# Order of the first loads, repeated-row loads for three vectors, and another place for batch 1's k, in a fused linear-attention and MLP-mixer kernel

## The chip, the cores and the metric

One core of one Trainium2 chip runs the whole program. The metric is the device time of one execution in microseconds (us), as the median of several runs.

## The reference

Linear attention without softmax over 8 batches, 8 heads, 576 tokens and 64 features a head, normalized to its root mean square, then a residual mixer (ResMLP with affine norms) with d_model 512 and a hidden width of 2048. Inputs and output are float32.

```python
kv = einsum('bhsd,bhse->bhde', k, v)
out = einsum('bhsd,bhde->bhse', q, kv)
x = out / sqrt(mean(out * out, -1) + 1e-6) * g_norm      # heads side by side: [b, s, 512]
a1 = alpha1 * x + beta1
tok = einsum('ts,bsd->btd', w_tok, a1)
u = x + lam * tok
a2 = alpha2 * u + beta2
ch = maximum(a2 @ w_ch1, 0) @ w_ch2
result = u + lam * ch
```

## The kernel before

**How the work is tiled.** Tokens lie on partitions, 128 at a time; 576 tokens make four tiles and a tail of 64, and the tails of two neighbouring batches share one tile (`xt`). Weights are cast to bf16 as they are loaded and stay in SBUF: `wt` is W_tok transposed, `w1` W_ch1 in four blocks of 512 hidden columns (L890 multiplies with it, a ReLU on ACT follows, L885), `w2` W_ch2 in four blocks (L915). These two, with `tok` (L789), are the main work of TensorE (PE): for each batch 16 groups of four L890, then 16 groups of four L915.

**Two streams on PE.** `mm` (L110) puts each group of matmuls in the list `main` (the two MLP layers, in fixed order) or `fill` (all the rest: attention, token mixing, transposes, for the batches to come). `schedule` (L122) is a planner written in the kernel: every operation has a cost that its author gave it, every load a size, and the planner runs a small model of five engines and one shared DMA stream. At each time it takes, on ACT, DVE, POOL and SP, the first operation by priority (`P.bias`, `pri`) that is ready in the model, and on PE a `fill` group if one is ready, woven matmul by matmul with a `main` group. What comes out is one fixed order for each engine (`self.sequence`), and `synchronize` (L257) puts semaphore waits where they are needed. On the chip every engine works through its order strictly: an instruction that waits holds up all behind it on its engine.

**Batch 0, the head of the program.** No main work is ready yet, so batch 0 is done in four pairs of heads. For each pair p: SP loads raw k and q (L486), POOL loads v, cast to the matmul type float32r (L478); POOL rounds k (`round_early`, L563) and copies q (`qt_early`, L574); PE transposes q (L580), ACT evicts it (L586); PE forms kv (`kv_early`, L613), DVE and ACT copy it into `kvc` (L624, L627); PE forms the output (`norm_pair`, L745, and the tail of 64 tokens in `norm_tail`, L764, for two pairs together). `norm_ops` follows: square on ACT (L695), reduce on DVE (L698), square root on ACT (L701), reciprocal on DVE (L704), and three DVE multiplications (L706 by the reciprocal, L710 into `rm` or `rtl`, which token mixing reads, L713 into `xt`); for the pairs the copy to `xm` is on ACT (L716) and its product with g_norm on POOL (L718). PE then mixes tokens (`tok_pair`, L804, 20 matmuls a pair), DVE adds (L812), PE transposes for the MLP (`a2_pair`, L843), and ACT applies alpha2 and beta2 on the way out (L847). The first main matmul needs all four pairs of this.

**Constants.** W_tok is loaded by POOL (L504, L506) after v of pair 0, and transposed on PE (L955, L957). Column sums of W_tok (L976, L978) spread beta1's part over rows. Six rows (alpha1, lam, beta1, alpha2, beta2, g_norm) are loaded by ACT's queue into one partition, in this order (L495, L497). DVE forms e1 = alpha1 * lam * g_norm * 8 and lam * beta1 there (L525 to L536). A row is spread over 128 partitions by a matmul with K=1 against a row of ones and an ACT copy: `broadcast` (L544, L547) for e1, g_norm, lam, alpha2 and beta2, `beta_rows` (L994, L998) for lam * beta1. A float32 matmul counts twice in the trace (two passes).

**Batch 1.** Its q and k are loaded by SP in two halves each, by the same `load_early`: k into the region of W_ch2 (`w2`), where batch 0's k was, q into `xm[2:4]`. ACT rounds this k (L566), POOL copies q. `w2` can be loaded (L1054) when those roundings are done. v of batch 1 follows on POOL's queue (`load_v(1, 0, 8)`), when PE has finished with batch 0's. Later batches are loaded by `load_kv` and `load_q`.

Of the kernel before, what the change touches and what calls it, by code (L numbers as in the profile page):

```python
# [17 lines left out]
DM = 512  # L18
# [34 lines left out]
class Prog:  # L53
    ENGINES = ("PE", "ACT", "DVE", "POOL")

    def __init__(self, nc, stack):
        self.nc, self.stack = nc, stack
        self.ops, self.lastw, self.readers = [], {}, {}
        self.ps = stack.enter_context(nc.psum_tensor("ps", [128, 8, 512], F32))
        self.eng = {"PE": nc.tensor, "ACT": nc.scalar, "DVE": nc.vector,  # L60
                    "POOL": nc.gpsimd, "SP": nc.sync}
        self.pools = {"main": (0, 1, 2, 3), "fill": (4, 5, 6, 7), "any": tuple(range(8))}
        self.main, self.fill = [], []
        self.bias = 0.0
        self.reach = 24

    def bank(self, pool):
        return Bank(self, pool)
# [41 lines left out]
    def mm(self, stream, cols, fns, r=(), w=(), slow=False, after=(), margin=0.3,  # L110
           urgent=False):

        n = len(fns)
        per = cols * MM_NS + 0.0025
        o = Op("PE", "w" if slow else "m", n * (max(per, 0.213 if slow == "r" else 0.109) if slow else max(per, 0.056)),
               0.24, fns, self.bias, len(self.ops))
        o.margin, o.narrow, o.urgent = 0.0 if urgent else margin, cols < 512, urgent
        (self.main if stream == "main" else self.fill).append(o)
        return self._add(o, r, w, after)


    def schedule(self):  # L122
# [50 lines left out]
        def take(o, t, cost=None):  # L173
            nonlocal dma_free, left
            for tile, b in zip(o.alloc, place(o, t)):
                tile.bank = b
                if owner[b] is not None:
                    o.deps.update(owner[b].ops)
                owner[b] = tile
            o.start = t  # L180
            if o.kind == "d":
                if o.nbytes > 0.25:
                    dma_free = max(dma_free, t + 1.4) + o.nbytes
                    o.end = dma_free + 1.6
                else:
                    o.end = t + 3.2
            else:
                o.end = t + (o.cost if cost is None else cost) + o.lat
            events.add(o.end)
            if o.margin:  # L190
                events.add(o.end + 0.3)
            left -= 1

        while left:
            moved = True
            while moved:
# [13 lines left out]
                if free["PE"] <= t + 1e-9:  # L210
                    m = main[0] if main and can(main[0], t) else None
                    f = None
                    for o in fill[:self.reach]:
                        if o.urgent or not (last_fill and m):
                            if can(o, t, o.margin if m else 0.0):
                                f = o
                                break
                    last_fill = False
                    if f is not None and m is not None and f.kind == "w" and m.narrow:
                        f = None  # L220
                    if f is not None and m is not None and f.kind == "w" and not f.urgent and not any(
                            x.pool == "any" for x in f.alloc):
                        fill.remove(f)
                        main.pop(0)
                        cost = sum(max(len(o.fns) * 0.056, (len(o.fns) * 0.075 if o is f else o.cost))
                                   for o in (f, m))
                        take(f, t, cost)
                        take(m, t, cost)
                        free["PE"] = t + cost
                        self.sequence.append((f, m))  # L230
                    elif f is not None:
                        fill.remove(f)
                        take(f, t)
                        free["PE"] = t + f.cost
                        self.sequence.append((f,))
                        last_fill = True
                    elif m is not None:
                        main.pop(0)
                        take(m, t)
                        free["PE"] = t + m.cost  # L240
# [130 lines left out]
def bass_transnormer_attn__then__resmlp_affine_kernel(  # L371
# [15 lines left out]
    with ExitStack() as stack:  # L387
# [46 lines left out]

        def f32(t, letters):
            return t[0:96].rearrange("p %s -> p (%s)" % (letters, letters)).bitcast(F32)
        sk = [six(f32(w2, "j f")[:, 0:3072])] * 2
        sq_ = six(xm[0:96, 2:4].rearrange("p b c f -> p (b c f)")[:, 0:3072])
        wl = hh[:, 6144:8448].rearrange("p (c s) -> p c s", c=4)
        wlt = hh[0:64, 8448:9024]  # L440
        rows = a2m[0:1].rearrange("p b j t -> p (b j t)").bitcast(F32).rearrange(
# [39 lines left out]
                w=[("v", p) for p in range(h0 // 2, h1 // 2)], after=after, issue=0.8)  # L481

        def load_early(b, h0, h1, what, after=()):
            for n, x, st in what:
                P.dma("SP", "%s%d_%d" % (n, b, h0), dcost(96 * (h1 - h0), 80),
                      lambda e, x=x, st=st: e.dma_start(  # L486
                          st[:, h0:h1].rearrange("p h c d -> p h (c d)"),
                          x[b, h0:h1].rearrange("h (p c) d -> p h (c d)", c=6)),
                      w=[("st", n, p) for p in range(h0 // 2, h1 // 2)],
                      after=after)  # L490

        for p in range(4):
            load_early(0, 2 * p, 2 * p + 2, (("k", k, sk[0]), ("q", q, sq_)))
        for i, x in enumerate((moe_alpha1, moe_lam, moe_beta1, moe_alpha2, moe_beta2)):
            P.dma("ACT", "row%d" % i, 0.2, lambda e, i=i, x=x: e.dma_start(  # L495
                rows[0:1, i, :], x[None, :]), w=[("row", i)], issue=0.3)
        P.dma("ACT", "row5", 0.1, lambda e: e.dma_start(rows[0:1, 5, 0:DH], g_norm[None, :]),  # L497
# [42 lines left out]
        def broadcast(i, dst, key, n=DM):  # L540
            t = P.bank("any")
            for f in range(0, n, 128):
                m = min(128, n - f)
                P.mm("fill", 512, [lambda e, f=f, m=m: e.matmul(  # L544
                    t.ap()[:, f:f + m], ones[0:1, :], rows[0:1, i, f:f + m], start=True,
                    stop=True)], r=[("row", i), "ones"], w=[t])
# [11 lines left out]

        def round_early(b, p):
            dst = kr6[:, p].rearrange("p c (h d) -> p h c d", h=2)  # L560
            src = sk[b][:, 2 * p:2 * p + 2]
            if b == 0:
                P.op("POOL", pool(768, 0), lambda e: e.tensor_copy(out=dst, in_=src),  # L563
                     r=[("st", "k", p)], w=[("k", p)])
            else:
                P.op("ACT", act(768), lambda e: e.activation(dst, src, ACT.Identity),  # L566
                     r=[("st", "k", p)], w=[("k", p)])

        def qt_early(b, p):
            s = p % 2  # L570
# [420 lines left out]
        def beta_rows():  # L991
            t = P.bank("any")
            for f in range(0, DM, 128):
                P.mm("fill", 512, [lambda e, f=f: e.matmul(  # L994
                    t.ap()[:, f:f + 128], ones[0:1, :], rows[0:1, 2, f:f + 128], start=True,
                    stop=True)], r=[("row", 2), "ones"], w=[t])
# [23 lines left out]
        for p in range(4):  # L1020
            P.bias = 10.0 * p + 10
            tok_pair(p)
            a2_pair(0, p)
        P.bias = 50.0
        broadcast(1, lam_bc, "lam")
        broadcast(3, a2_bc, "a2")
        broadcast(4, b2_bc, "b2")


        def alias(new, old):  # L1030
            for key in new:
                for o in old:
# [7 lines left out]
        rws = [("row", i) for i in range(6)]  # L1040
        alias([("a2m", i, c) for i in (1, 2) for c in range(4)], rws)
        P.readers.setdefault(("a2m", 0, 0), [])

# [15 lines left out]
        def load_q(b, after=()):  # L1059

            for g in range(4):
# [1 line left out]
                P.dma("SP", "q%d" % g, dcost(2304, 25), lambda e, hp=hp, j=j, g=g: e.dma_start(  # L1063
                    qs[32 * g:32 * g + 32, 0:2304].rearrange("p (m d) -> p m d", d=32),
                    q[b, 4 * hp:4 * hp + 4, :, 32 * j:32 * j + 32].rearrange(
                        "h (k t) d -> t (h k) d", t=32)), w=[("qs", g)], issue=0.7,
                    after=after)

        def load_kv(b, after=()):
# [29 lines left out]

        def attention(b):  # L1100
            P.bias = 100.0 * b
            if b == 1:
                for p in range(4):
                    round_early(1, p)
                alias([("w2", i) for i in range(4)], st("k"))
                for i in range(4):
                    load_w2(i, landed("k", 3))
                kv_early(1, [0, 1, 2, 3])
                for p in range(4):
                    qt_early(1, p)  # L1110
# [13 lines left out]
            if b + 1 < NB:  # L1124
                load_kv(b + 1)
                if b == 1:
                    late = [P.lastw[("w2", 2)][0]]
                    load_early(2, 0, 4, (("q", q, sq_),), late)
                    load_early(2, 4, 8, (("q", q, sq_),), late)
# [68 lines left out]
```

## Time and profile before

| what | value |
|---|---|
| three runs | 374.86, 377.99, 377.81 us |
| median | 377.81 us |
| the profiled execution's own time | 375.4 us |
| its span in the profile | 373.4 us |
| PE, DVE, ACT, POOL busy | 357.8, 183.0, 161.9, 154.4 us |
| granted TensorE clock | 0.999 |
| DMA | 46.5 MB moved, 38.04 MB read from HBM |

A profile line such as `9.42 0.68 PE L544 MATMUL ps<-a2m,ones 1*128 1x64 f32 x2 [2.46 <-DVE a2m L528]` reads: from 9.42 us, for 0.68 us, two matmuls of line 544; ahead of them PE idled 2.46 us, which the DVE instruction of line 528 ended. In the chain of waits a line gives start, length, and the engine and line that the end of the program hung on. A line of the load table gives destination and source, the issuing queue, the number of loads, the size at the destination, and last the time from issue to landing in us. The rows lie in the tile `a2m`, batch 0's and batch 1's k in `w`, W_tok in `hh`.

### The profile page before, as it was taken

What the parts mean: (1) busy time and instruction counts of PE and PEld (TensorE: products, weight loads), DVE (VectorE), ACT (ScalarE), POOL (GpSimd) and SP (SyncE); (2) the same over time, 40 slices, a digit from 0 to 9 for tenths busy, and PEclk for the clock granted to TensorE, in tenths of its full rate; (3) what the DMA queues carried; (4) which work ended last, traced back from release to release, by engine and by line L of the source; (5) the groups of instructions that cost most, each with busy time, mean ns of one, the idle gap of its engine ahead of it and who ended that gap; (6) DMA issues with size and microseconds to landing.
All of it is one profiled execution on the core that took longest, in us unless ns stands there. A gap on an engine that the chain in (4) does not pass through costs nothing.

```text
span 373.4 us, 5300 instructions
## 1 busy us (share of the span) xinstructions
PE 357.8 (96%) x2118; PEld 208.9 (56%) x2118; DVE 183.0 (49%) x335; ACT 161.9 (43%) x323; POOL 154.4 (41%) x150
## 2 busy tenths in 40 slices
PE   0999999899999999999999999999999999999995
PEld 0869876367657644654567455446546444444642
DVE  4147708721893598269519936953962120020042
ACT  1355787335683325451568205821564006206500
POOL 7342481015407835923870398148219430130000
PEclk9999999999999999999999999999999999999999
DMA  8969999999909793993899199903202221020012
GB/s 199 245 113 256 136 151 213 275 160 166 246 2 120 146 285 66 142 255 105 115 167 185 38 163 217 174 15 87 70 2 42 58 84 29 4 82 28 2 56 84
DMA packets 95716, 46.50 MB, mean 125 GB/s; under 512 B 68735, under 2 KB 91079, under 8 KB 95692
## 3 DMA queue, kind: packets, MB, share of 16 engines
q1 hardware_dynamic: 70400, 24.78, 37.8%
q0 software_dynamic: 25264, 21.38, 34.0%
q8 instruction: 16, 0.26, 0.3%
q14 instruction: 8, 0.07, 0.1%
q10 hardware_dynamic: 28, 0.01, 0.0%
HBM read 38.04 MB, written 9.44 MB: 127 GB/s over the span
## 4 chain that ended last, share of the span: by engine, by line
PE 88%; DVE 7%; DMA 2%; ACT 2%; issue 1%; ACTq 0%; DVEq 0%
PE ps L915 32%; PE ps L890 25%; PE ps L789 8%; PE ps L900 4%; PE ps L639 3%; PE ps L580 2%; PE ps L613 2%; PE ps L730 2%; DVE ps L706 2%; DMA a2m<-in_g_norm_dram 2%; PE ps L823 1%; PE ps L804 1%; DVE rm L710 1%; PE ps L644 1%; PE ps L544 1%; PE ps L745 1%
## 5 line engine op out<-in xcount | busy, mean ns | idle before, releaser
L915 PE MATMUL ps<-w,hh 128*128 128x512 bf16 x576 | 139.1, 381 | 0.0
L890 PE MATMUL ps<-a2m,w 128*128 128x512 bf16 x512 | 122.9, 381 | 0.0
L885 ACT ACTIVATE hh<-ps 128x512 bf16<-128x512 f32 x144 | 85.1, 596 | 85.3 <-PE ps L890 75.7
L915 PEld LDWEIGHTS ps<-w,hh 128*128 128x128 bf16 x576 | 55.2, 98 | 59.5 <-issue 0.4
L890 PEld LDWEIGHTS ps<-a2m,w 128*128 128x128 bf16 x512 | 48.9, 98 | 53.6 <-issue 0.4
L936 POOL TENSOR_TENSOR xm<-xm,tmp 128x512 f32<-128x512 f32 x28 | 35.5, 1269 | 72.8 <-DVE tmp L931 72.6
L931 DVE TENSOR_TENSOR tmp<-ps,lam_bc 128x512 f32<-128x512 f32 x36 | 24.8, 690 | 79.4 <-PE ps L915 78.9
L875 POOL TENSOR_TENSOR a1f<-xm,a_bc 128x512 f32<-128x512 f32 x24 | 30.3, 1276 | 44.1 <-DVE xm L796 44.0
L730 PE MATMUL ps<-kvc,qt 128*128 128x128 f32 x140 | 40.0, 395 | 0.0
L698 DVE TENSOR_REDUCE small<-sq 128x8 f32<-128x512 f32 (+2 forms) x41 | 26.8, 659 | 23.2 <-ACT sq L695 23.1
L695 ACT ACTIVATE sq<-ps 128x512 f32<-128x512 f32 (+2 forms) x41 | 23.6, 581 | 28.3 <-PE ps L730 24.9
L878 POOL TENSOR_TENSOR a2b<-a1f,b_bc 128x512 bf16<-128x512 f32 x27 | 34.0, 1278 | 0.3
L796 DVE TENSOR_TENSOR xm<-ps,xm 128x512 f32<-128x512 f32 x28 | 19.2, 687 | 22.5 <-PE ps L789 22.4
L789 PE MATMUL ps<-rm,wt 128*128 128x512 bf16 x112 | 28.8, 379 | 1.3 <-DVE rtl L710 1.3
L730 PEld LDWEIGHTS ps<-kvc,qt 128*128 128x128 f32 x140 | 27.1, 199 | 2.0
L706 DVE TENSOR_TENSOR ps<-ps,small 128x512 f32<-128x512 f32 (+2 forms) x41 | 27.2, 676 | 0.5
L710 DVE TENSOR_TENSOR rm<-ps,e_bc 128x512 bf16<-128x512 f32 x32 | 21.4, 676 | 0.1
L639 PE MATMUL ps<-vr,kr 128*128 128x128 f32 x96 | 20.2, 336 | 0.0
L574 POOL COPY qp<-xm 96x768 f32<-96x768 f32 x12 | 9.8, 831 | 23.4 <-DMA xm<-in_q_dram 23.4
L789 PEld LDWEIGHTS ps<-rm,wt 128*128 128x128 bf16 x112 | 10.5, 98 | 14.4 <-DVE rtl L710 3.1
L713 DVE TENSOR_TENSOR xm<-ps,g_bc 128x512 f32<-128x512 f32 x28 | 18.2, 675 | 0.1
L639 PEld LDWEIGHTS ps<-vr,kr 128*128 128x128 f32 x96 | 17.3, 194 | 1.8
(104 smaller groups left out, 331.4 us busy)
## 6 DMA issues: line engine op xcount, KB each, us to landing
out_dram<-xm SPq DMA_DIRECT2D x32, 256.0 KB, 2.0
kr<-in_k_dram POOLq DMA_DIRECT2D x6, 1024.0 KB, 7.7
vr<-in_v_dram POOLq DMA_DIRECT2D x6, 1024.0 KB, 9.9
qs<-in_q_dram SPq DMA_DIRECT2D x20, 288.0 KB, 5.9
w<-in_moe_w_ch_dram POOLq DMA_DIRECT2D x8, 512.0 KB, 8.9
xm<-in_q_dram SPq DMA_DIRECT2D x4, 576.0 KB, 11.5
w<-in_k_dram SPq DMA_DIRECT2D x4, 288.0 KB, 9.8
xm<-in_q_dram SPq DMA_DIRECT2D x4, 288.0 KB, 11.5
```

The costliest lines, as they stand in the source:

```text
L639: fns += [lambda e, t=t, c=c, h=h, o=o: e.matmul(t.ap()[:, o], kr4[:, h, c:c + 2, :].rearrange("p c d -> p (c d)"), vr4[:, h, c:c + 2, :]. ...
L698: P.op("DVE", dve(n), lambda e: e.tensor_reduce(out=st, in_=sq[rs, s3, 0:nst, :], axis=AX.X, op=ALU.add), r=[("sq", s3)], w=[("sm", s4)])
L706: P.op("DVE", dve(n), lambda e: e.tensor_tensor(out=grp(ps()), in0=grp(ps()), in1=st[..., None].to_broadcast([rs.stop - rs.start, nst, DH] ...
L710: P.op("DVE", dve(n), lambda e: e.tensor_tensor(out=r, in0=shape(ps()), in1=e1, op=ALU.mult), r=[t, "e1"], w=rks, pri=-10)
L730: P.mm("fill", 128, [lambda e, p=p: e.matmul(dst(p), qt[:, p, cs], kvc[:, i, p, :], start=(p == 0), stop=(p == 3)) for p in range(4)], r=[ ...
L789: P.mm("fill", 512, [lambda e, sc=sc: e.matmul(t.ap(), wt[:, sc if sc < 4 else tw(b), 128 * c:128 * c + 128], rsrc(b, sc, al), start=(sc = ...
L875: P.op("POOL", pool(512), lambda e: e.tensor_tensor(out=a1f[:, s], in0=x, in1=a2_bc[:], op=ALU.mult), r=ks + ["a2"], w=[("a1f", s)])
L878: P.op("POOL", pool(512), lambda e: e.tensor_tensor(out=a2b[:, c], in0=a1f[:, s], in1=b2_bc[:], op=ALU.add), r=[("a1f", s), "b2"], w=[("a2 ...
L885: P.op("ACT", act(512), lambda e: e.activation(dst, t.ap(), ACT.Relu), r=[t], w=keys, pri=-1000)
L890: P.mm("main", 512, [lambda e, dj=dj: e.matmul(t.ap(), w1[:, dj, 128 * fj:128 * fj + 128], a2m[:, b % 3, dj, :], start=(dj == 0), stop=(dj ...
L915: P.mm("main", 512, [lambda e, fj=fj, t=t, c=c: e.matmul(t.ap(), (ht[:, fj, 128 * c:128 * c + 128] if c < 4 else hl[:, fj, :]), w2[:, fj, ...
L936: lambda e: e.tensor_tensor(out=x, in0=x, in1=tmp[:, s], op=ALU.add),
```

## The change

- On POOL's queue W_tok comes first; v of pair 0 is loaded raw by SP (third, after the first k and q) into a corner of `qs` and rounded by ACT into `vr`.
- alpha2, beta2 and lam are no longer spread by K=1 matmuls. SP loads each straight into 128 partitions, reading the same row 128 times, after W_ch1's second block has landed. The rows alpha2 and beta2 leave ACT's queue; lam's row stays, since e1 needs it.
- Batch 1's k goes to `xm[:, 1]` and `tmp` in place of the region of W_ch2. Its loads and those of batch 1's q wait for the last q of batch 0, and stand ahead of the W_ch1 blocks 1 to 3 in the list; W_ch2's first block waits for the first half of batch 1's k, the others for its second.
- The planner's figures change: K=1 matmuls cost 0.25, PE's groups cost twice (slow ones 1.25 times) up to 36 us of model time, POOL's loads land later. With them the order of the instructions on every engine changes, most in the first 60 us. In it, batch 1's four ACT roundings stand between the pairs of batch 0, all 24 transposes of batch 1's q stand ahead of the first main matmul, and batch 1's kv matmuls after eight groups of the main stream.

```diff
@@ planner
+        self.warm = 36.0
-        o = Op("PE", ... n * (max(per, 0.213 if slow == "r" else 0.109) ...
+        o = Op("PE", ... n * (max(per, {"r": 0.213, "k": 0.25}.get(slow, 0.109)) ...
-                    o.end = dma_free + 1.6
+                    o.end = dma_free + (1.6 if o.q == "SP" else 3.6 if t < 20 else 2.0)
+        def cold(o, t):
+            if t > self.warm:
+                return o.cost
+            return o.cost * (2.0 if o.kind == "m" else 1.25)
...
-                        take(f, t)
-                        free["PE"] = t + f.cost
+                        c = cold(f, t)
+                        take(f, t, c)
+                        free["PE"] = t + c
@@ where raw k and v lie
-        sk = [six(f32(w2, "j f")[:, 0:3072])] * 2
+        k0s = six(f32(w2, "j f")[:, 0:3072])
+        k1s = [t[0:96].rearrange("p c f -> p (c f)")[:, 0:1536].rearrange(
+            "p (h c d) -> p h c d", h=4, c=6) for t in (xm[:, 1], tmp)]
+        def sk(b, h0, h1):
+            if b == 0:
+                return k0s[:, h0:h1]
+            return k1s[h0 // 4][:, h0 % 4:(h1 - 1) % 4 + 1]
+        sv = qs[0:96, 0:768].rearrange("p (h c d) -> p h c d", h=2, c=6)
@@ first loads
         for p in range(4):
-            load_early(0, 2 * p, 2 * p + 2, (("k", k, sk[0]), ("q", q, sq_)))
-        for i, x in enumerate((moe_alpha1, moe_lam, moe_beta1, moe_alpha2, moe_beta2)):
+            load_early(0, 2 * p, 2 * p + 2, (("k", k), ("q", q)))
+            if p == 0:
+                P.dma("SP", "v0_0", dcost(96 * 2, 80), lambda e: e.dma_start(
+                    sv[:, 0:2].rearrange("p h c d -> p h (c d)"),
+                    v[0, 0:2].rearrange("h (p c) d -> p h (c d)", c=6)), w=["sv"])
+        for i, x in enumerate((moe_alpha1, moe_lam, moe_beta1)):
...
-        load_v(0, 0, 2)
         P.dma("POOL", "wl", dcost(512, 106), lambda e: e.dma_start(
...
+        P.op("ACT", act(768), lambda e: e.activation(vr6[:, 0:2], sv, ACT.Identity),
+             r=["sv"], w=[("v", 0)])
...
-        P.bias = 50.0
-        broadcast(1, lam_bc, "lam")
-        broadcast(3, a2_bc, "a2")
-        broadcast(4, b2_bc, "b2")
@@ loads after batch 0
-        load_w1(0, landed("k", 3))
-        load_w1(1, landed("q", 3))
-        first = [P.lastw[("w1", 0)][0]]
-        load_early(1, 0, 4, (("k", k, sk[1]), ("q", q, sq_)), first)
-        load_early(1, 4, 8, (("k", k, sk[1]), ("q", q, sq_)), first)
-        load_v(1, 0, 8)
-        load_w1(2, landed("q", 1))
-        load_w1(3, landed("q", 3))
+        k3, q3 = landed("k", 3), landed("q", 3)
+        load_w1(0, k3)
+        load_early(1, 0, 4, (("k", k), ("q", q)), q3)
+        load_w1(1, q3)
+        load_w1(2, q3)
+        load_v(1, 0, 8)
+        load_early(1, 4, 8, (("k", k), ("q", q)), q3)
+        load_w1(3, q3)
+        alias([("w2", i) for i in range(4)], st("k"))
+        for i in range(4):
+            load_w2(i, landed("k1", 3) if i else landed("k1", 1))
+        for x, dst, key in ((moe_lam, lam_bc, "lam"), (moe_alpha2, a2_bc, "a2"),
+                            (moe_beta2, b2_bc, "b2")):
+            P.dma("SP", key, dcost(128, 86), lambda e, x=x, dst=dst: e.dma_start(
+                dst[:], x[None, :].to_broadcast([128, DM])), w=[key],
+                after=[P.lastw[("w1", 1)][0]])
@@ attention(1)
-                alias([("w2", i) for i in range(4)], st("k"))
-                for i in range(4):
-                    load_w2(i, landed("k", 3))
+                alias([("x", 1, c, p) for c in range(4) for p in range(4)], st("k1")[0:2])
+                alias([("tmp", i) for i in range(3)], st("k1")[2:4])
```

More of the change, by code (lines that the diff above doesn't have):

```diff
@@ L114, in mm @@
         per = cols * MM_NS + 0.0025
-        o = Op("PE", "w" if slow else "m", n * (max(per, 0.213 if slow == "r" else 0.109) if slow else max(per, 0.056)),
+        o = Op("PE", "w" if slow else "m", n * (max(per, {"r": 0.213, "k": 0.25}.get(slow, 0.109)) if slow else max(per, 0.056)),
                0.24, fns, self.bias, len(self.ops))
@@ L238, in schedule @@
                         main.pop(0)
-                        take(m, t)
-                        free["PE"] = t + m.cost
+                        c = cold(m, t)
+                        take(m, t, c)
+                        free["PE"] = t + c
                         self.sequence.append((m,))
@@ L483, in load_early @@
         def load_early(b, h0, h1, what, after=()):
-            for n, x, st in what:
+            for n, x in what:
+                st = sk(b, h0, h1) if n == "k" else sq_[:, h0:h1]
                 P.dma("SP", "%s%d_%d" % (n, b, h0), dcost(96 * (h1 - h0), 80),
                       lambda e, x=x, st=st: e.dma_start(
-                          st[:, h0:h1].rearrange("p h c d -> p h (c d)"),
+                          st.rearrange("p h c d -> p h (c d)"),
                           x[b, h0:h1].rearrange("h (p c) d -> p h (c d)", c=6)),
-                      w=[("st", n, p) for p in range(h0 // 2, h1 // 2)],
+                      w=[("st", n + "1" * (n == "k" and b), p)
+                         for p in range(h0 // 2, h1 // 2)],
                       after=after)
         for p in range(4):
-            load_early(0, 2 * p, 2 * p + 2, (("k", k, sk[0]), ("q", q, sq_)))
-        for i, x in enumerate((moe_alpha1, moe_lam, moe_beta1, moe_alpha2, moe_beta2)):
+            load_early(0, 2 * p, 2 * p + 2, (("k", k), ("q", q)))
[4 more added lines that the diff above has]
+        for i, x in enumerate((moe_alpha1, moe_lam, moe_beta1)):
             P.dma("ACT", "row%d" % i, 0.2, lambda e, i=i, x=x: e.dma_start(
@@ L545, in broadcast @@
                     t.ap()[:, f:f + m], ones[0:1, :], rows[0:1, i, f:f + m], start=True,
-                    stop=True)], r=[("row", i), "ones"], w=[t])
+                    stop=True)], r=[("row", i), "ones"], w=[t], slow="k")
             P.op("ACT", act(n), lambda e: e.activation(dst[:], t.ap()[:, 0:n], ACT.Identity),
@@ L560, in round_early @@
             dst = kr6[:, p].rearrange("p c (h d) -> p h c d", h=2)
-            src = sk[b][:, 2 * p:2 * p + 2]
+            src = sk(b, 2 * p, 2 * p + 2)
             if b == 0:
@@ L566, in round_early @@
                 P.op("ACT", act(768), lambda e: e.activation(dst, src, ACT.Identity),
-                     r=[("st", "k", p)], w=[("k", p)])
+                     r=[("st", "k1", p)], w=[("k", p)])
         def qt_early(b, p):
@@ L995, in beta_rows @@
                     t.ap()[:, f:f + 128], ones[0:1, :], rows[0:1, 2, f:f + 128], start=True,
-                    stop=True)], r=[("row", 2), "ones"], w=[t])
+                    stop=True)], r=[("row", 2), "ones"], w=[t], slow="k")
             for i, h in ((0, 64), (1, 0)):
@@ L1039, in bass_transnormer_attn__then__resmlp_affine_kernel @@
               ["wl", "wlt"])
-        rws = [("row", i) for i in range(6)]
+        rws = [("row", i) for i in (0, 1, 2, 5)]
         alias([("a2m", i, c) for i in (1, 2) for c in range(4)], rws)
@@ L1065, in load_q @@
                     q[b, 4 * hp:4 * hp + 4, :, 32 * j:32 * j + 32].rearrange(
-                        "h (k t) d -> t (h k) d", t=32)), w=[("qs", g)], issue=0.7,
+                        "h (k t) d -> t (h k) d", t=32)), r=["sv"], w=[("qs", g)], issue=0.7,
                     after=after)
@@ L1127, in attention @@
                     late = [P.lastw[("w2", 2)][0]]
-                    load_early(2, 0, 4, (("q", q, sq_),), late)
-                    load_early(2, 4, 8, (("q", q, sq_),), late)
+                    load_early(2, 0, 4, (("q", q),), late)
+                    load_early(2, 4, 8, (("q", q),), late)
                 else:
```

## The prediction

> **What bounds the kernel now.** I read the page's busy shares first, then the chain of work that ended last over the first 60 us, then each engine's timeline there, and last the landing times of single loads.
>
> ```profile
> span 373.4 us, 5300 instructions
> PE 357.8 (96%) x2118; PEld 208.9 (56%) x2118; DVE 183.0 (49%) x335; ACT 161.9 (43%) x323; POOL 154.4 (41%) x150
> PE   0999999899999999999999999999999999999995
> ```
>
> TensorE is busy 96% of the span. PE's list of waits holds only four: 6.2 and 2.5 us before 9.42, 0.9 at 43, and 1.3 later. So time can come only from the first 50 us: from idle there, or from PE work taken away. The chain in that stretch:
>
> ```profile
> 2.56 6.61 DMA a2m<-in_g_norm_dram
> ...
> 10.11 1.47 PE ps L613 x6
> ...
> 33.07 1.57 PE ps L544 x6
> 34.65 1.71 PE ps L804 x15
> ...
> 41.66 0.92 DVE ps L706 x2
> ...
> 43.56 2.41 PE ps L804 x40
> ...
> 49.66 0.87 PE ps L890 x4
> ```
>
> Three parts: the g_norm row lands at 9.17; PE then works without a gap until 38.0; then the normalization of head pair 3 runs over ACT and DVE until `rtl` at 43.5. The first main matmul (L890) starts at 49.50. Nearly all that follows is PE work, so I price the change by where that start goes. PE's timeline, then ACT's:
>
> ```profile
> 24.22 1.91 PE L976 MATMUL ps<-wt,pick 128*128 128x512 bf16 x4
> 41.05 1.60 PE L544 MATMUL ps<-a2m,ones 1*128 1x128 f32 x12
> 43.56 0.40 PE L804 MATMUL ps<-rm,wt 128*128 128x128 bf16 x4 [0.90 <-DVE rtl L710]
> ```
>
> ```profile
> 43.70 1.56 ACT L566 ACTIVATE kr<-w 96x768 fp32r<-96x768 f32 x2
> ```
>
> This line is batch 1's k, rounded on ACT behind the whole chain. The loads of batch 1's k and q by SP (issued from 24.89 on), and W_ch1's second block on POOL's queue (issued 25.73), with us to landing last:
>
> ```profile
> w<-in_k_dram SPq DMA_DIRECT2D x1, 576.0 KB, 4.9
> xm<-in_q_dram SPq DMA_DIRECT2D x1, 576.0 KB, 8.6
> w<-in_k_dram SPq DMA_DIRECT2D x1, 576.0 KB, 11.7
> xm<-in_q_dram SPq DMA_DIRECT2D x1, 576.0 KB, 18.1
> w<-in_moe_w_ch_dram POOLq DMA_DIRECT2D x1, 512.0 KB, 13.0
> ```
>
> The W_ch1 block came last into an empty queue of its own and still took 13.0, where an undisturbed block (issued 19.50) took 5.4: the queue that starts second is held up.
>
> **The change, part by part.** I use the order of the built program on each engine, with durations from the profiled execution.
>
> *Head, on PE.* alpha2's and beta2's rows leave ACT's queue, so g_norm lands fourth, not sixth. Beta (third) landed at 5.4 and g_norm at 9.17, 1.24 a row, which gives 6.7; the record of landings has the fourth row at 5.76. I take 5.8, the row that stood there; the other end costs 0.9. DVE scales it (0.18) and PE starts at 6.05. The work PE had done by 16.3 is g 0.68, kv of pair 0 1.47, e1 2.00, transposes 1.15, beta 0.79 + 1.57: 7.7 in all, so it ends at 13.75.
>
> Pair 0's v now comes raw over SP in third place, where k of pair 1 landed at 10.1, and ACT rounds it (0.83, as L566) after e1's eviction: done by 11.9, and PE wants it at 12.3. Hidden by e1 and the transposes; without that cover, up to 1. W_tok landed at 14.8 and 15.6 behind 288 KB of v; without it I take 13.4, a wait of 0 (1.8 if it comes no earlier). Each later SP tile lands a place later, about 2 us (q of pair 3 at 21.4 for 20.1); PE wants that at 26.7.
>
> From 13.75 PE does W_tok's transposes 3.46, norm pairs 0 and 1 2.50, transposes of q for pairs 1 to 3 3.11, kv of 1 to 3 3.93, column sums 2.65: 29.4. Pairs 2 and 3 (1.06 each) end at 31.5; before, pair 3 ended at 37.4. Of these 5.9, 2.6 are the earlier start, 1.6 the lam broadcast, 1.7 the 15 L804 that now stand behind pair 3.
>
> *The broadcasts.* 12 K=1 matmuls (24 passes) go: 1.57 + 0.93 + 1.60 = 4.1 on PE. Only the 1.57 was on the chain; the others ended in PE's 0.90 wait for `rtl`. Three ACT copies (0.6 each) go with them. The repeated-row loads are 256 KB each; by the packets of the trace SP's loads alone ran at some 250 KB/us (and W_ch blocks alone at 200), so 1 us each. They queue behind batch 1's k and q and are wanted some 30 us later: nothing.
>
> *Batch 1's k, on ACT.* Its four rounding steps (0.83 each) now stand inside batch 0's chain: two ahead of pair 2's square, two behind it and ahead of pair 2's square root. The last two read k's second half. SP starts the four loads when q of pair 3 has landed (21.4). Before, the third landed 12.6 after the first was issued: 34.0. ACT is there at about 32.2. Behind the waiting step are pair 2's root, all of pair 3's, and DVE, which needs the roots. Ends: 30.6 (the pace of the first two, no wait) and 39.6 (held up by 5.6, as the W_ch1 block, whose first packets came 5.6 after its issue). I take 34.0, the same loads in the same order.
>
> From there: two roundings to 35.7, root 0.25; then on DVE, pair 2's reciprocal 0.2, L706 0.7, pair 3's reduce 0.65, L710 0.65, tok add 0.69, reciprocal and the tail's reduce 0.55, L706 0.67, the tail's reciprocal 0.15, L710 0.65, tok add 0.69, tail 0.35 + 0.40: `rtl` at 42.4, for 43.5 before. So the head's 5.9 becomes 1.1: ACT and DVE bind, not PE.
>
> *PE until the main stream.* Seven groups of L804 end at 35.5, then PE waits for the tok add at 38.9, and fills with q transposes. After `rtl`: 40 L804 2.41, transposes 0.44 + 0.50 + 0.46 with 0.1 of waits, eviction 0.77: 47.2, if PE runs at the speed that it had from 38.2. Before 38.2 it ran at half: 128x512 matmuls came every 0.43 at 24.2 (0.22 in the main stream) and L804 every 0.114 until 38.2, then 0.056, though the granted clock reads 1.00 throughout and PE had no gap from 9.42. The rise came 3.5 after the first L804. If the 3.4 gap loses it and the next L804s win it back as late, main starts at 49.2. The only gap after the rise, 0.90, lost nothing; 3.4 lies far beyond it: I take the middle, 48.2, and keep both ends.
>
> The Trainium skill (TensorE: Matmul & The Clock Gate, Part 1) puts the rise after about 3.4 us of sustained activity and the fall after an idle window of that length. Its rise disagrees with this trace (28 gapless us at half speed); by its fall, which speaks against the change, main starts at 49.2 and the gain is 0.3; by the short gap, 47.2 and 2.3.
>
> Of the work left beside the main stream, before had 6 kv matmuls and 15 transposes, after 24 kv matmuls and no transpose: at 0.075 and 0.083 each 1.7 and 1.8, equal.
>
> *Later loads.* PE's kv of batch 1 now stands after eight groups of L890 (8 x 0.86): about 55. Its v waits on POOL's queue behind four W_ch1 blocks and one of W_ch2 (512 KB, 2.6 each) and takes 5.4; with SP's 9.4 between, 50 to 53. Covered by 2 us or more. Batch 2's q follows W_ch2's third block (about 59). At SP's full pace it lands at 66 to 68, and PE wants its copies at about 68.5: 0.2 of wait. Before, q had 10 us to spare here.
>
> **Sum.** 49.5 - 48.2 = 1.3 won, 0.2 lost: 1.1. The profiled run took 375.4 (span 373.4 and 2.0 around it), so 374.3 on its terms. The three runs read 374.86, 377.81, 377.99, so the profiled one lies 2.4 below their median. I put the median after at 375.2, between 374.3 and 376.7.
>
> **Rivals.**
> - *A, slower: SP's k loads are held up.* POOL's first W_ch1 block is issued at about 21, 0.4 before SP's first k; if POOL's queue starts first and SP's waits the 5.6 that W_ch1's second block waited, k's second half lands at 39.6. For it: that row. Against: then SP came first. The chain moves 5.6: 374.3 + 5.6 = 379.9. It decides from a landing at 35.1 on.
> - *B, slower: batch 2's q is late.* Its loads took 14.3 before, beside k and v of batch 2. From 59: 73.3, PE stands 5.6 past 67.7 (copy included), DVE's norm chain hides 1.1 of it: 374.1 + 4.5 = 378.6. Against: POOL's queue is nearly empty at 60.
> - *C, faster: neither the k wait nor the cold clock.* k lands by 32.2, the chain gains 1.8, the clock stays: main at 45.4, 374.3 - 2.8 = 371.5. For it: SP alone moved its first halves in 4.9 and 8.6.
> - *D, no change:* the clock falls and W_tok comes no earlier; main at 49.2 to 49.5, 375.4.
>
> **How the numbers follow.** Forecast 0.34, A 0.18, B 0.12, C 0.20, D 0.16. About 1% (3.8 us) is what a measurement of this kernel can tell from none. C passes it (3.9 won) and A does (4.5 lost); B (3.2) does where q is a little later still, half of its cases: faster 0.20, slower 0.18 + 0.06 = 0.24, same the remaining 0.56. The range, 371 to 380, takes in C, both ends of the clock, and A up to its price.
>
> **What would show it.** Right: first matmul near 6; pair 3's L745 near 32 to 33; a wait on ACT at its third rounding of batch 1's k, near 32; `rtl` near 42; first L890 near 48; no PE wait for v or q of batch 2 above 1 us. Wrong: ACT's wait over 3 us or none, L804 at 0.114 after 43, or PE waiting on a DMA past 50.

## The result and the profile after

The kernel after took 379.1 us as a median (376.86 to 381.46, 20 runs), the kernel before, run beside it, 377.45 (374.86 to 379.32, 20 runs). The ratio is 1.006, with a 95% interval of 1.0034 to 1.0086. It became slower, where 1.1 us of gain was forecast. The profiled executions stand 2.2 apart (377.64 and 375.4; spans 375.8 and 373.4), and it is between these two that the time is followed below.

The page of the kernel after (line numbers of after are those of before plus 21 from L504 to L1003, and plus 17 from L1048 on):

```profile
span 375.8 us, 5270 instructions
PE 355.9 (95%) x2094; PEld 207.6 (55%) x2094; DVE 182.9 (49%) x335; ACT 162.8 (43%) x321; POOL 153.7 (41%) x149
PE   2997899999999969999999999999999999999995
```

PE has 1.9 us less work than before (355.9 for 357.8), and yet the span is longer. Look at the slices: two of PE's digits behind the first are under 9 in the head, as one would look for them, but a 6 stands at the fifteenth, 131 to 141 us, in the middle of the main stream, where the kernel before has only nines.

The chain of waits in the head:

```profile
21.36 11.55 DMA tmp<-in_k_dram
32.93 1.57 ACT kr L587 x2
34.51 0.20 ACT small L722
...
36.85 0.61 DVE xm L833
37.51 0.66 PE ps L864 x4
...
46.88 7.08 PE ps L911 x32
```

In this execution the head does what the prediction said, only quicker: batch 1's k lands at 32.9, ACT rounds it inside batch 0's chain, and the first main matmul starts at 46.88, 2.6 earlier than before (49.50). If nothing else had happened, the span would be 370.8.

The four longest of PE's list of waits, with total, number and longest:

```profile
PE ps L565 <- DVE a2m L549: 6.7, 1, 6.7
PE ps L810 <- DVE rtl L731: 3.7, 1, 3.7
PE ps L864 <- DVE xm L833: 1.9, 1, 1.9
PE ps L911 <- ACT a2m L868: 1.2, 1, 1.2
```

The second line is new at this place and length: before, the same matmuls (L789) waited 1.3 for `rtl` in all, 1.1 of it at 70. PE's timeline there, first after, then before:

```profile
134.44 2.98 PE L936 MATMUL ps<-w,hh 128*128 128x512 bf16 x13
141.16 1.89 PE L810 MATMUL ps<-rm,wt 128*128 128x512 bf16 x4 [3.74 <-DVE rtl L731]
142.84 0.63 PE L810 MATMUL ps<-rtl,wt 128*128 128x512 bf16 x1
...
148.11 2.12 PE L911 MATMUL ps<-a2m,w 128*128 128x512 bf16 x9
```

```profile
135.75 3.84 PE L915 MATMUL ps<-w,hh 128*128 128x512 bf16 x17
139.43 2.75 PE L890 MATMUL ps<-a2m,w 128*128 128x512 bf16 x12
142.25 1.04 PE L789 MATMUL ps<-rm,wt 128*128 128x512 bf16 x4
```

Before, when batch 1's second MLP layer (L915) ran out, twelve main matmuls of batch 2 (L890) came first, and batch 3's token mixing (L789) behind them. After, the token mixing (L810) stands first, in an order that is fixed, and needs `rtl`, the last product of batch 3's normalization. PE stands 3.74 us, with work behind the waiting instruction that could have run. And the wait has a second price. By stage (length, busy time of PE, PEld, DVE, ACT and POOL, each with its number of instructions, then the granted clock, the DMA share and GB/s):

```profile
38.00:42.00 4.00, 4.00 (x32) 4.00 (x30) 2.84 (x7) 3.42 (x8) 3.00 (x4) 0.57 1.20 238
...
138.00:140.00 2.00, 0.00 (x0) 0.00 (x0) 1.96 (x4) 0.00 (x0) 1.26 (x1) 1.00 0.23 88
140.00:144.00 4.00, 2.84 (x7) 1.04 (x8) 3.62 (x6) 1.34 (x2) 0.00 (x0) 0.57 0.30 68
144.00:148.00 4.00, 4.00 (x24) 1.66 (x22) 3.50 (x6) 1.34 (x2) 3.64 (x3) 1.00 0.00 0
```

In the four us around the end of the wait the granted clock is 0.57: half speed for 3.4 us. The first four L810 took 1.89 where they take 1.03 at full speed. The whole block, 141.16 to 148.11, took 6.95; at the pace of before's rows (1.08 for five matmuls, so 4.3 for the four groups, and 1.2 for the tail) it would be 5.5. So the clock cost 1.4.

The sum: 2.6 won in the head, 3.74 + 1.4 = 5.1 lost at 141, together 2.5 more; the spans differ by 2.4.

### The profile page after: what moved, and what is told of

Same layout as the page of the kernel before. It is cut to its first block, busy times and chain, and to the rows that moved or that the text cites. A ratio compares the mean times of both kernels' runs of the same rounds, so it can differ in the third digit from the quotient of the medians.

```text
span 375.8 us, 5270 instructions
## 1 busy us (share of the span) xinstructions
PE 355.9 (95%) x2094; PEld 207.6 (55%) x2094; DVE 182.9 (49%) x335; ACT 162.8 (43%) x321; POOL 153.7 (41%) x149
## 3 DMA queue, kind: packets, MB, share of 16 engines
q0 software_dynamic: 25056, 21.08, 32.3%
## 4 chain that ended last, share of the span: by engine, by line
PE 81%; DMA 7%; DVE 7%; ACT 1%; SPq 1%; issue 1%; DVEq 0%
PE ps L911 30%; PE ps L936 29%; PE ps L810 8%; DMA xm<-in_q_dram 4%; PE ps L921 4%; DMA tmp<-in_k_dram 3%; PE ps L660 3%; PE ps L751 2%; DVE ps L727 2%; DVE small L719 1%; SPq L503 1%; PE ps L844 1%; DVE rm L731 1%; PE ps L665 1%; PE ps L601 1%; PE ps L864 1%
## 5 line engine op out<-in xcount | busy, mean ns | idle before, releaser
L936 PE MATMUL ps<-w,hh 128*128 128x512 bf16 x576 | 138.2, 381 | 0.0
L936 PEld LDWEIGHTS ps<-w,hh 128*128 128x128 bf16 x576 | 55.0, 98 | 59.8 <-issue 0.4
L911 PEld LDWEIGHTS ps<-a2m,w 128*128 128x128 bf16 x512 | 48.7, 98 | 54.9 <-ACT a2m L868 1.4
L716 ACT ACTIVATE sq<-ps 128x512 f32<-128x512 f32 (+2 forms) x41 | 23.5, 581 | 31.5 <-PE ps L751 30.5
L810 PE MATMUL ps<-rm,wt 128*128 128x512 bf16 x112 | 29.9, 391 | 3.7 <-DVE rtl L731 3.7
L1088 POOL DMA_DIRECT2D kr<-in_k_dram x6 | 5.6, 926 | 43.9 <-PE ps L665 24.3
L810 PEld LDWEIGHTS ps<-rm,wt 128*128 128x128 bf16 x112 | 11.1, 100 | 17.9 <-DVE rtl L731 4.2
L1101 ACT ACTIVATE qt<-qp 128x576 fp32r<-128x576 f32 x20 | 13.6, 682 | 15.6 <-DVE qp L1098 15.6
```

Of the source, the lines that this page charges most:

```text
L810: P.mm("fill", 512, [lambda e, sc=sc: e.matmul(t.ap(), wt[:, sc if sc < 4 else tw(b), 128 * c:128 * c + 128], rsrc(b, sc, al), start=(sc = ...
L911: P.mm("main", 512, [lambda e, dj=dj: e.matmul(t.ap(), w1[:, dj, 128 * fj:128 * fj + 128], a2m[:, b % 3, dj, :], start=(dj == 0), stop=(dj ...
L936: P.mm("main", 512, [lambda e, fj=fj, t=t, c=c: e.matmul(t.ap(), (ht[:, fj, 128 * c:128 * c + 128] if c < 4 else hl[:, fj, :]), w2[:, fj, ...
```

## The experiments

Theory 1: the planner's new order costs the time, by putting batch 3's token mixing ahead of batch 2's main matmuls. Theory 2: the work that ran beside the main stream has lost its lead (batch 1's kv starts at 53.6 instead of about 46), and a wait comes back wherever one is taken away. A third, for the runs that need it: the new loads themselves cost time. In some kernels a helper `reorder` moves instructions within one engine's finished list; the semaphore waits are placed after it. The line numbers shift with each edit: L810 of after (L789 of before) is L841 in the run in before's order, L833 in the one with batch 4's loads moved, and L811 in the one with the dependency.

### One move, the place of the wait

```diff
         P.schedule()
+        P.reorder("PE", batch 3's four tok groups and tail, behind=third L911 group of batch 2)
```

> The changed kernel, with one edit in TensorE's fixed order: token mixing of batch 3 (four groups and the tail) stands behind the first three groups of batch 2's main matmuls (12 L911) instead of ahead of them. Nothing else moves. Theory 1 (the order): in the changed kernel TensorE idled 3.7 us at 137.4 for batch 3's rtl while the transposed a2 of batch 2 had landed at 137.2, and the clock then fell to half for 3.4 us; both go, so about 5 us less than the changed kernel, 370 to 372 where that one took 375.8 in span, and faster than the kernel before by about 1%. Theory 2 (the lead is gone): the filling work runs some 8 us later against the main stream than before, so the wait turns up again at a later batch and the time stays within 1.5 us of the changed kernel.

Measured: 375.52 us, ratio to before 0.9973 (0.9944 to 1.0002). The wait for `rtl` and the half clock at 141 are gone, and with them 3.6 of the time of after (379.1). At 140 a wait for batch 2's transposes shows in its place, without a clock drop:

```profile
PE ps L935 <- DMA a2m<-a2b: 1.2, 1, 1.2
```

Theory 1 carries, with 3.6 of the 5 us that it gave; theory 2 (within 1.5 of the kernel after) does not hold. Between the profiled executions the span fell from 375.8 to 373.9, where 370 to 372 was forecast. What is missing is the 1.2 at 140, and the head, where nothing was moved: the main stream began at 48.7, 1.9 later than in the profile of after.

### ACT's roundings behind the chain

```diff
+        P.reorder("ACT", last two roundings of batch 1's k, behind=last square root of batch 0)
```

> The changed kernel, with ACT's last two roundings of batch 1's k moved behind batch 0's last square root; nothing else moves. The square root of pair 2 no longer waits for the load (1.16 us) nor for two roundings (1.57 us), so batch 0's chain should end about 1.9 us sooner and the main stream start about 1.5 us sooner (46.9 to about 45.4). Theory 1: this is won at the end too, less a wait for batch 1's v, which landed at 53.1 and would then be wanted at 52.1: 0.5 to 1.5 us less than the changed kernel. Theory 2: all of it is lost again at batch 3's token mixing, whose wait grows from 3.7 to about 5 us: the same time as the changed kernel.

Measured: 377.66, ratio 1.0032 (1.0008 to 1.0056). The main stream starts at 45.1, 1.8 earlier than in the profile of after; the wait for `rtl` stays at 3.7, where theory 2 had 5. The interval overlaps that of after (1.0034 to 1.0086), so this pair alone does not give the size. The same move gave 1.8 on top of the first one (375.52 to 373.72, below) and 2.3 on top of the dependency (375.41 to 373.15, below).

The size changes from one execution to the next, because the landing of k's second half does. Four of the kernels here have the same order in the head. ACT's wait in the run with batch 4's loads moved, in after, in the run above and in the one with the dependency:

```profile
32.40 1.57 ACT L610 ACTIVATE kr<-tmp 96x768 fp32r<-96x768 f32 x2 [0.63 <-DMA tmp<-in_k_dram]
32.93 1.57 ACT L587 ACTIVATE kr<-tmp 96x768 fp32r<-96x768 f32 x2 [1.16 <-DMA tmp<-in_k_dram]
34.78 1.57 ACT L610 ACTIVATE kr<-tmp 96x768 fp32r<-96x768 f32 x2 [2.60 <-DMA tmp<-in_k_dram]
34.36 1.58 ACT L588 ACTIVATE kr<-tmp 96x768 fp32r<-96x768 f32 x2 [2.42 <-DMA tmp<-in_k_dram]
```

Their main streams began at 46.42, 46.88, 48.74 and 49.78, so the 2.6 that after won in the head is what one execution had. The wait that the prediction made its main term is real, but it isn't what made the kernel slower.

### Both moves

> The changed kernel with both edits: ACT's last two roundings of batch 1's k behind batch 0's last square root, and batch 3's token mixing behind the first three groups of batch 2's main matmuls. Theory 1: the two gains add, 6 us less than the changed kernel, about 1.2% faster than the kernel before. Theory 2: no more than 1.5 us less than the changed kernel.

Measured: 373.72, ratio 0.9913 (0.9886 to 0.994), faster than either kernel. What is left in the middle:

```profile
PE ps L937 <- DMA a2m<-a2b: 2.8, 1, 2.8
```

With the head 1.8 earlier, PE is at batch 2's main matmuls before batch 2's transposes have landed.

### The repeated-row loads alone, in the kernel before

The kernel before with lam, alpha2 and beta2 loaded into 128 partitions, their broadcasts gone, and the planner left to order what remains.

```diff
-        broadcast(1, lam_bc, "lam")
-        broadcast(3, a2_bc, "a2")
-        broadcast(4, b2_bc, "b2")
+        (three P.dma("SP", ...) with x[None, :].to_broadcast([128, DM]), and two rows fewer on
+         ACT's queue, as in the change)
```

> The kernel before with one part of the change alone: lam, alpha2 and beta2 spread by repeated-row loads on SP instead of K=1 matmuls, and two rows fewer on ACT's queue, with the planner's old figures. Theory 1: 4.1 us of TensorE work go; the earlier g_norm and the 1.57 us on the chain give 1.5 to 3 us less than the kernel before, if the new order holds no wait. Theory 2: the main stream gets ahead of the filling work and the gain is given back at a later batch: within 1 us of the kernel before.

Measured: 385.04, ratio 1.0243 (1.0199 to 1.0288). Taking 4.1 us of work from PE made the kernel 7.7 us slower. From PE's waits and from its timeline:

```profile
PE ps L789 <- DVE rtl L710: 7.6, 2, 6.4
PE ps L804 <- DVE rtl L710: 2.8, 1, 2.8
```

```profile
147.09 1.89 PE L789 MATMUL ps<-rm,wt 128*128 128x512 bf16 x4 [6.45 <-DVE rtl L710]
```

The same line waits for the same product at the same place as in the kernel after, here for 6.4 us, and the clock is at half for 6.8 around its end (143.6 to 150.4).

### The same operations in before's order

The planner plans the kernel before as it is; then the broadcasts are taken out of the finished lists and the loads put in.

```diff
         P.schedule()
+        P.replace(gone=K=1 matmuls and ACT copies of lam, alpha2, beta2 and the rows of the last two,
+                  loads=three repeated-row loads on SP, behind=batch 1's second q load)
```

> The kernel before, its written order kept on every engine exactly as planned with the broadcasts in it; then the K=1 broadcasts of lam, alpha2 and beta2 with their three ACT copies are taken out of it, repeated-row loads by SP stand behind batch 1's second q load in their place, and alpha2's and beta2's row loads go from ACT's queue. The same operations as in the run where the planner was left free to order them anew (385.0 us), so the two differ in order alone. Theory 1 (the new order is what costs time): PE loses 4.1 us of work, 1.6 of it on the chain of the head, and g_norm comes up to 2.5 earlier; no wait for rtl at batch 3's token mixing, and 372 to 376 us, at least 9 below the free order. Theory of the loads (the loads or the missing PE work themselves cost it, by transfers that collide or a clock that falls in the idle that the broadcasts filled): 380 or more.

Measured: 376.38, ratio 0.9998 (0.9964 to 1.0032). Same operations, same loads, and 8.7 us less than in the free order: the loads are not what costs. But the 372 to 376 that theory 1 gave is missed by a little. The profiled execution is one of the two slowest of twelve (380.1), so its waits show where 4.1 us less of PE work can go, and not what the median lost:

```profile
PE ps L856 <- DVE rtl L762: 2.6, 1, 2.6
PE ps L665 <- POOL kr L615: 2.5, 1, 2.5
PE ps L665 <- DMA vr<-in_v_dram: 2.0, 1, 2.0
```

PE now comes too early for batch 0's rounded k, for `rtl` of the head (ready at 41.5, 2.0 earlier than before), and for batch 1's v. All its waits add up to 14.6, those of before to 10.9: the broadcasts had filled time that PE would have waited in any case. In this execution the clock was at half from 46.5 to 56.7 as well. The theory of the loads had named such a drop in idle that the broadcasts filled, so that part of it is real in this execution; the median is 3.6 below the 380 or more that it gave.

### The planner's old figures in the kernel after

```diff
-        max(per, {"r": 0.213, "k": 0.25}.get(slow, 0.109))
+        max(per, 0.213 if slow == "r" else 0.109)
-        o.end = dma_free + (1.6 if o.q == "SP" else 3.6 if t < 20 else 2.0)
+        o.end = dma_free + 1.6
         def cold(o, t):
+            return o.cost
```

> The kernel after with the planner's old figures (K=1 cost, landing allowance and the cold head factors put back), all its loads and operations as they are; only the order can differ. If the new figures are what puts batch 3's token mixing ahead of batch 2's first main matmuls, the wait of 3.7 us and the half clock of 3.4 us at 141 go and it runs in 374 to 376 us. If the missing work and the earlier main stream do that whatever the figures (theory 1 as the free order of the rows alone has it), the wait stays, there or elsewhere, and it runs in 378 us or more.

Measured: 380.59, ratio 1.009 (1.0065 to 1.0116), with a wait of 6.4 for `rtl` that ends at 143.8:

```profile
PE ps L808 <- DVE rtl L729: 7.3, 2, 6.4
```

The new figures did not bring the bad order; with the old ones it is worse.

### Why the order changed

The two kernels differ one step earlier. (What made the planner choose differently there was not followed further.) PE's timeline of before, then of after:

```profile
111.97 1.03 PE L789 MATMUL ps<-rm,wt 128*128 128x512 bf16 x4
...
118.04 0.30 PE L639 MATMUL ps<-vr,kr 128*128 128x128 f32 x1
```

```profile
111.54 0.31 PE L660 MATMUL ps<-vr,kr 128*128 128x128 f32 x1
...
115.88 1.04 PE L810 MATMUL ps<-rm,wt 128*128 128x512 bf16 x4
```

Before, batch 2's token mixing comes ahead of batch 3's kv (L639); after, behind it. Kv frees the buffers for batch 4's k and v, token mixing frees POOL's work on batch 2's alpha2 and beta2. POOL's timeline of before, then of after, shows what follows:

```profile
114.02 2.58 POOL L875 TENSOR_TENSOR a1f<-xm,a_bc 128x512 f32<-128x512 f32 x2 [16.17 <-DVE xm L796]
...
126.30 0.95 POOL L1071 DMA_DIRECT2D kr<-in_k_dram  x1
```

```profile
116.25 0.89 POOL L1088 DMA_DIRECT2D kr<-in_k_dram  x1 [18.31 <-PE ps L665]
...
118.69 2.53 POOL L896 TENSOR_TENSOR a1f<-xm,a_bc 128x512 f32<-128x512 f32 x2
```

Batch 4's k and v now go out ahead of batch 2's products. In the planner's model, which has one transfer stream for all queues, batch 2's transposes then stand behind batch 4's q, k and v. These are the model's own times, made when the kernel is built, not times of the chip:

```
planned                         before    after
batch 4's first k load          117.9     113.2
batch 2's last transpose lands  125.0     144.6
batch 2's first main matmul     130.4     144.6
batch 3's first token mixing    133.0     137.7
PE idle ahead of these          0         3.4 and 1.5
```

With main matmuls not ready until 144.6 in the model, token mixing at 137.7 is the right choice. The plans of the two other kernels with the long wait (the row loads alone, and the old figures) have 5.5 of PE idle ahead of batch 3's token mixing. On the chip the last two transposes were issued from 133.4 on and landed by 137.2, just as L936 ran out at 137.4. The order was right for transfers that the chip doesn't have.

### Batch 4's loads behind batch 2's products, by hand

```diff
+        P.reorder("POOL", batch 4's four k and v loads, behind=last a2b product of batch 2)
```

> The kernel after with one move: batch 4's four k and v loads stand on POOL's queue behind the last product of batch 2's alpha2/beta2 step, as in the kernel before (there they were issued at 126 us; after, at 117, beside batch 4's q on SP's queue, and batch 2's transposes, queued on SP behind that q, were issued at 130 to 135 for 118 to 125 before). Theory 1 (at 141 us PE waits for rtl of batch 3 because the order puts its token mixing first; batch 2's transposes are not what it waits for): the transposes land some 8 us earlier and the time stays at 379, within 1. Theory of the queue (the late transposes are the cause): the wait of 3.7 us and its clock drop go, 374 us.

Measured: 379.64, ratio 1.0064 (1.0036 to 1.0093): no change. The transposes do go earlier, as SP's timeline shows, first after, then this kernel:

```profile
114.17 8.62 SPq L1080 DMA_DIRECT2D qs<-in_q_dram  x4
122.83 7.22 SPq L960 DMA_DIRECT2D out_dram<-xm  x1
130.10 1.33 SPq L902 DMA_TRANSPOSE a2m<-a2b  x1
...
133.41 2.53 SPq L902 DMA_TRANSPOSE a2m<-a2b  x2
```

```profile
113.71 6.18 SPq L1103 DMA_DIRECT2D qs<-in_q_dram  x4
121.95 1.31 SPq L983 DMA_DIRECT2D out_dram<-xm  x1
123.30 2.61 SPq L925 DMA_TRANSPOSE a2m<-a2b  x2
```

With k and v on POOL's queue at the same time, one store on SP's queue took 7.2 us to issue behind four q loads, for 1.3 without, and the transposes stand behind the store. But PE's wait is for `rtl` and stays:

```profile
140.69 1.89 PE L833 MATMUL ps<-rm,wt 128*128 128x512 bf16 x4 [3.73 <-DVE rtl L754]
```

As theory 1 has it, the late transposes are not what PE waits for in the kernel after.

### The three moves together

> Three moves in the kernel after: batch 3's token mixing behind batch 2's first three main groups, ACT's last two roundings of batch 1's k behind batch 0's last root (these two together ran in 373.7 us, with PE waiting 2.8 us for batch 2's transposes at 139 and 3.4 us of half clock behind that), and batch 4's k and v loads behind batch 2's products on POOL's queue. If the transposes are late because they stand on SP's queue behind batch 4's q, which shares the 16 DMA engines with batch 4's k and v, both the 2.8 and some 1.5 of the clock go: 369.5 us. If another link (DVE's tok adds, POOL's products, the later k and v) takes their place, 373 or more.

Measured: 373.31, ratio 0.9894 (0.9869 to 0.992). PE's wait for the transposes, 2.8 with two moves, is nearly gone, and the granted clock of the profiled execution stays full from the head on:

```profile
PE ps L938 <- DMA a2m<-a2b: 0.7, 1, 0.7
```

The wait went as the first theory has it, and no other link stands in its place at 140 (0.2 for `rtl`), but the time is what the second one gave, 373 or more. The span of the profiled execution fell from 374.3 to 371.5, though its main stream began 0.9 later (46.0), behind a wait of 0.8 for W_tok. The median fell by 0.4 only, for a gain of 4 expected: of the eleven executions with two moves ten ran at a granted clock of 0.997 or more, in 372.0 to 374.2, and the profiled one, at 0.995, in 376.2. I had priced the move against the one execution that lost its clock.

### One dependency in the plan

Instead of moves by hand, the planner is told what it needs to choose well:

```diff
-                load_kv(b + 1)
+                load_kv(b + 1, [P.last[b - 1, 3]] if b + 1 == 4 else ())   # last a2b product of batch 2
```

> The kernel after, with one dependency more in the plan: batch 4's k and v loads wait for batch 2's last alpha2/beta2 product, and the planner orders everything with that. In its own plan of the kernel after, the four loads go ahead of those products, its single transfer channel then has batch 2's transposes land at 144.6, and it puts batch 3's token mixing first, with PE idle for 3.4 and 1.5 us; with the dependency the plan has no idle there and batch 2's main matmuls first. Theory 1, with the loads' place as what moved the order: the wait for rtl of 3.7 us and 1.4 us of half clock at 141 go, 374.0 us, under before. Theory of the lead (what is lost is the time that filling work ran ahead of the main stream): the wait comes back at another place, 377 or more.

Measured: 375.41, ratio 0.9964 (0.9938 to 0.999), 3.7 under the kernel after (3.6 by the two ratios). PE's timeline has batch 2's main matmuls first again, as before, and no wait there:

```profile
137.33 2.98 PE L937 MATMUL ps<-w,hh 128*128 128x512 bf16 x13
140.15 4.48 PE L912 MATMUL ps<-a2m,w 128*128 128x512 bf16 x20
144.67 1.04 PE L811 MATMUL ps<-rm,wt 128*128 128x512 bf16 x4
```

It is 1.4 above the expectation. In the head of the profiled execution (376.11) k landed at 34.4, PE idled 3.0 from 36 on and lost its clock for 6.8 us, so that the main stream began at 49.8.

### The dependency and the roundings

> The same dependency, and ACT's last two roundings of batch 1's k behind batch 0's last root. By theory 1 the head gives the 1.5 to 1.8 us by which main started earlier with that move (45.1 for 46.9): 372.3 us, at or under the 373.3 of the three moves by hand. Otherwise 374 or more.

Measured: 373.15, ratio 0.9905 (0.9879 to 0.993), 0.9 above the expectation and level with the three moves by hand. The head's clock holds and main starts at 45.25. This is the fastest version tried, with the 373.3.

### The dependency beside the row loads alone

> The kernel before with the repeated-row loads instead of the broadcasts, ordered anew (385.0 us, with a wait of 6.4 us for rtl at 147 and 6.8 us of half clock after it), and the same dependency. By theory 1 the wait and the 3.4 us that the half clock cost go: 375 us, about the time of before and of the run that kept before's order (376.4). If the new order costs time mostly elsewhere (waits of 2.8 at 42 and 1.1 at 73 stay), 380 or more.

Measured: 379.08, ratio 1.0067 (1.0038 to 1.0096). Of the 385.0 of the free order 6.0 are gone, for 10 expected: batch 3's wait for `rtl` is 1.3 instead of 6.4, the longest of three:

```profile
PE ps L790 <- DVE rtl L711: 2.5, 3, 1.3
```

The waits of 2.8 at 42 and 1.1 at 73 stay, so it fell between the two expectations, and 2.7 to the run in before's order are left. The profiled execution (376.96) kept a full clock; the other eleven had 0.988 to 0.995 and 377.4 to 381.4. That the clock lost in the head makes up the rest is likely, but only argued: no other profile of this kernel was taken.

## Why the prediction was wrong

- **The failing step** is "Nearly all that follows is PE work, so I price the change by where that start goes", with the check on it, "Of the work left beside the main stream ... equal". It counted the work behind the start and not its order. The planner orders everything anew, and at 137 us put an instruction that had to wait ahead of ones that hadn't. In the profiled execution that cost 5.1 us, 3.74 of waiting and 1.4 of clock, more than the 2.6 that the head won. The order of the built program, which the prediction used for the head, shows the token mixing ahead of the twelve main matmuls; it was not read so far.
- **The range.** The 379.1 lies inside the 371 to 380 by luck: the range reached up to 380 for rival A, whose late k did not come. And the 1% that was taken as the least that a measurement can tell was too coarse: 20 runs of each kernel told 0.6% from none.
- **The head's terms** were right in kind. PE began at 6.70 (6.05 predicted) and found W_tok there. Pair 3's L766 ended at 32.3 (31.5). Batch 1's k landed at 32.9 (34.0), ACT waited 1.16 for it, and `rtl` was ready by 40.6 (42.4). The start of the main stream gained 2.6 (1.3). In the four profiles with this order of the head k landed at 32.4 to 34.8 and the main stream began at 46.4 to 49.8, so the 34.0 and the 48.2 of the prediction lie among them.
- **The clock** did fall in the gap, which was 1.93 long instead of 3.4: half speed from 38.07 to 41.48. It had also risen earlier, at about 34.65: four L825 took 0.63 to 0.65 until then and 0.39 after, while the granted clock reads 1.00. The middle value that was taken, 48.2, was 1.3 late. That the next gap could lie beyond the head was not thought of.
- **The broadcasts**, "Only the 1.57 was on the chain", holds only as far as `rtl`, which came 2.0 earlier in the profile with the order kept. It was not a gain in time: PE then waited 2.0 for batch 1's v, and the median gained nothing that can be measured (0.9998, 0.9964 to 1.0032).
- **Rival A** (k held up to 39.6) did not come, nor **B**: batch 2's q landed at 62.5 and 64.5, and PE's waits there, 0.74 and 0.33, ended on DVE and ACT; before, it had waited 1.11 for `rtl` at about the same time. **C** needed neither the wait for k nor the half clock, and in the profile of after both came (1.16 and 3.4); its start of 45.4 was reached only with the roundings moved (45.1). **D** had half of its condition: the clock fell, but W_tok was there in time. None named the wait at 141, and the list of what would show the prediction wrong had only waits on a DMA past 50 in it; this one was on DVE.

## What to carry to other kernels

Where a planner orders the work, taking work away is a change of the whole order: 4.1 us less on TensorE made this kernel 7.7 us slower, and the same operations in the old order ran in the old time. Before pricing such a change, follow the new order of the bottleneck engine to the end, look where two streams cross, and ask of each instruction that now stands first whether what it reads is ready; the plan's own idle time, new at one place, would have pointed to it. One profile is one execution: the same order of the head began its main stream anywhere from 46.4 to 49.8. And a dependency that says what must not overtake what keeps the planner from a choice that only its model of the transfers makes good.

## What the runs showed of the hardware

- **The clock after waits of PE** (behind the first 35 us). Waits of 1.4 us or less did not lower the granted clock, unless several came close together (1.16, 0.60 and 0.70, from 35.2 to 39.3, in the run with the old figures). Of eight waits of 1.9 to 3.0 in the profiles, six were followed or accompanied by a drop. Two were not: 2.63 at 41 in the run in before's order, and 2.75 at 42 in the row loads with the dependency, where the same wait in the free order had one (half from 41.2 to 44.6). The five of 3.7 and 6.4 all had one, and the same wait of 3.7 brought 3.4 us of half speed in one profile and 6.8 in two. Half speed lasted 3.4, 6.8 or 10.2 us, always a multiple of 3.41 (the drop that each program has at its end left out). The Trainium skill (TensorE: Matmul & The Clock Gate, Part 1) has a free-running window of 3413 ns, which these lengths agree with, and would let the clock fall after an idle window of that length; here 1.93 of idle was enough.
- **One queue beside another.** A store on SP's queue, behind four q loads, took 7.2 us to issue while k and v moved on POOL's queue (8.6 with the first two moves), and 1.3 when they did not; the transposes stood behind it.
